# A second batch of attention in half heads, paired with the first

## The chip, the cores and the metric

The kernel runs on one core of a Trainium2 chip. The metric is device time in microseconds (us) of one execution. The engines are named as in the profile: PE (matrix multiply; PEld is its weight load), DVE (vector), ACT (scalar, activations), POOL (GpSimd) and SP (which issues DMAs). Each engine works through its own instructions in a fixed order and waits on semaphores for the others.

## The reference, cut to what matters

Eight batches of eight heads, 576 positions, head dimension 64. Attention with a decay, its output laid out as 4608 rows of 512, then two dense layers with a hard swish between:

```python
scores = scale * np.matmul(q, k.transpose(0, 1, 3, 2))
cum = np.cumsum(np.log(np.clip(f, 0.0001, 1.0)), axis=-1)
scores = np.where(causal, -1000000000.0, scores + cum[..., :, None] - cum[..., None, :])
attn = np.exp(scores - np.max(scores, axis=-1, keepdims=True))
attn = attn / (np.sum(attn, axis=-1, keepdims=True) + 1e-09)
x = np.matmul(attn, v).transpose(0, 2, 1, 3).reshape(B * S, H * D)
h = x @ w_in                                   # 512 -> 2048
g = h * np.clip(h + 3.0, 0.0, 6.0) / 6.0
return (g @ w_out).astype(np.float32)          # 2048 -> 512
```

The weights arrive in 64-bit floats and are decoded on the chip.

## The kernel before, in words

**Visits.** The program is one loop (L959) over a list of visits, `VH` (L96). A visit of kind "A" takes the first 256 query rows of two heads of batch 0 at once (4 visits). Kind "B" takes the other 320 query rows of one head of batch 0 (8 visits). Kind "F" takes a whole head; batches 1 to 7 go so (56 visits).

**Halves, A and B.** `natural` (L477) multiplies queries and keys once in float32 and takes each row's maximum on DVE (L493). `max_rows` turns the maxima into a row and sends it by DMA into the query tile. `scores` (L544) then computes the scores with keys on the partitions, in two matmuls (L551, L552) and a mask (L554), and ACT takes the exponential into a float32 tile. `av` (L682) multiplies this with V in float32 (L705). Each such matmul shows as two records. Its V is the unsplit one, and it reads a window of `NAV = 96` columns of it, which holds the head's 64 columns and its column of ones.

**Whole heads, F.** `rows` (L594) computes scores with queries on the partitions (L611, L614), takes the maximum on DVE while copying (L622), the exponential on ACT (L634), then splits the result into two float16 halves (L648, L651, L657, L662) and transposes it by DMA (L669). `av` multiplies it with a V that `v_split` has split into float16 halves (L694 to L699).

**The dense layers** come in units, a queue `units` that `done` (L936) fills when the eight heads (or the four pairs) of a batch are through and moved by `x_move` into a tile `xT` of 512 rows. `moe_in` computes h in 16 units (`h_unit`, L770: three float16 matmuls for each of four chunks, then L783, L786, L787, L788), `moe_out` the output in units of 128 rows (`out_unit`, L819: L824 to L826, accumulated over all 16 chunks). Batch 0 does this for its first 256 rows and then for the next 256; other batches for 512 rows at once. 64 rows of each batch are left, and two batches' rests go together (`rest_in`, `rest_out`). Two PSUM buffers (`ps_m`, L763) serve the h and output units, from batch 1 on also a third.

**Weights.** `w_in_work` and `w_out_work` are generators of about 85 steps: load, decode (L251 to L253), sum of squares, scale, split into float16 halves (L284, L287, L288, L295). Each visit takes `W_RATE` of them: 8 in A, 5 in B, 4 in F. The output units of batch 0 first run out what is left of them (L847).

**Order.** In each visit eight calls of `fill` (L925) put units in between the attention's instructions; a call earns `F_RATE` units (0.6 in B, 0.45 in batch 1, 1.06 later). Inputs are loaded three visits ahead, and copies to float32r tiles are made on POOL two ahead. The weighted sum of a visit is issued at the end of the next one, and `x_move` follows one visit later still. A scheduler with a model of the engines then fixes each engine's order.

Of the kernel before, what the change touches and what calls it, by code (L numbers as in the profile page):

```python
# [20 lines left out]
def kernel(  # L21
# [95 lines left out]
    def init_qk(i, eng):  # L117
# [5 lines left out]

    NAV = 96
    pav = ps_a.tile([P, NCH, NAV], F32, name="pav")

# [11 lines left out]

    v0 = [
        v16.bitcast(F32).rearrange("p n c j e -> p (n c j e)")[:, 0:3 * VR],  # L140
        xT[1].bitcast(F32).rearrange("p a c l t -> p (a c l t)")[:, 0:2 * VR],
    ]
    v0 = [t.rearrange("p (c e) -> p c e", e=VR) for t in v0]

    def v_parts(b):
        return v0 if b == 0 else [vst[:, 0:3], vst[:, 3:]]

    def v_chunk(b, c):
        return v_parts(b)[c // 3][:, c % 3]

# [199 lines left out]
    def load_v(b):  # L350
        src = vS[b]
        lo, hi = v_parts(b)
        with pinned() if PIN_V else nullcontext():
            if b == 0:
                nc.sync.dma_start(lo, src[0:3 * P].rearrange("(c p) e -> p c e", p=P))
                nc.sync.dma_start(hi[:, 0], src[3 * P:4 * P])
                nc.sync.dma_start(hi[:64, 1], src[4 * P:S])
            else:
                for p in (0, 64):
                    nc.sync.dma_start(vst[p:p + 64, 0], src[0:64])  # L360
                nc.sync.dma_start(vst[:, 1:], src[64:].rearrange("(c p) e -> p c e", p=P))

    def v_scale(b):
        pm = p2.tile([P, 2], F32, tag="pm", name=f"vm{b}")
# [8 lines left out]
        nc.vector.tensor_tensor(pm, pm, pm, op=ALU.mult)  # L373
        nc.vector.tensor_tensor(pm[:, 0:1], pm[:, 0:1], pm[:, 1:2], op=ALU.max)
        yield from pow2_scale(pm[:, 0:1], SV + b, IV + b, f"v{b}")
# [15 lines left out]
    def v_split(g):  # L391
        b, hp = divmod(g, NPAIR)
        t = v16[:, g % NV16]
        if g < NPAIR + NV16:
# [280 lines left out]

    def window(head):

        o = head % H * (D + 1)
        w0 = min(o, VR - NAV)
        return w0, o - w0  # L680

    def av(v, ph):  # L682
# [4 lines left out]
        if kind == "F":  # L687
            jh = n % 2
            blk = [(n, c, c) for c in range(NCH)]
            vh, vl = vt[:, :, jh, 0:D + 1], vt[:, :, jh, D + 1:VW]  # L690
            for c in range(NCH):
                pb = ph[:, HT[c]:HT[c] + (2 * c + 1) * P].rearrange("p (g t) -> p g t", t=P)
                o1, o0 = pav[:, c, 0:D + 1], pav[:, c, 0:D]
                nc.tensor.matmul(o1, pb[:, c], vh[:, 0], start=True, stop=False)  # L694
                nc.tensor.matmul(o0, pb[:, c], vl[:, 0], start=False, stop=(c == 0))
                for k in range(1, c + 1):
                    nc.tensor.matmul(o1, pb[:, c + k], vh[:, k], start=False, stop=False)
                    nc.tensor.matmul(o0, pb[:, c + k], vl[:, k], start=False, stop=False)  # L698
                    nc.tensor.matmul(o1, pb[:, k - 1], vh[:, k], start=False, stop=(k == c))  # L699
        else:  # L700
            blk = blocks(v)
            for head, c, pl, m, js in blk:
                w0, _ = window(head)
                for jc, o, kk in js:
                    nc.tensor.matmul(  # L705
                        pav[:m, pl, :], ph[:kk, o:o + m], v_chunk(b, jc)[:kk, w0:w0 + NAV],
                        start=(jc == 0), stop=(jc == c),
                    )
# [7 lines left out]
        for head in heads:  # L716
# [3 lines left out]
            c0, c1 = mine[0][1], mine[-1][1] + 1  # L720
            vo = window(head)[1] if b == 0 else 0
            rs = p2.tile([P, NCH, 1], F32, tag="rs", name=f"rs_{v}_{jh}")[:, p0:p1]
            total = pav[:, p0:p1, vo + D:vo + D + 1]
            if b == 0:

# [6 lines left out]
            nc.vector.tensor_tensor(  # L732
                xf[:, c0:c1, jh * D:(jh + 1) * D], pav[:, p0:p1, vo:vo + D],
                rs.to_broadcast([P, p1 - p0, D]), op=ALU.mult,
# [7 lines left out]
    def x_move(v):  # L742
# [12 lines left out]
        nc.sync.dma_start_transpose(  # L755
            xT[b % 2][:, cc, o:o + c1 - c0].rearrange("p c a t -> p (c a) t"),
            xhl[:, c0:c1].rearrange("p c a e -> p (c a e)"),
# [11 lines left out]

    def h_unit(x, fc, c0, c1, b, three, name):  # L770

# [3 lines left out]
        for cc in range(NCC):  # L775
# [6 lines left out]
        r = p2.tile([P, TT], F32, tag="rt", name=f"r_{name}_{fc}_{c0}", bufs=3)[:, :nw]  # L782
        nc.scalar.activation(  # L783
            r, ph, AF.Relu, bias=bias_r, scale=scol(A1 + NG * b + fc * NG // NFC)
        )
        nc.vector.scalar_tensor_tensor(r, r, 6.0 * CG, ph, op0=ALU.min, op1=ALU.mult)  # L786
# [49 lines left out]

    def moe_in(b, c0=0, c1=TT):

        for fc in range(NFC):
            j, new = divmod(fc, NFC // NG)  # L840
            if new == 0 and c0 == 0:
                while j not in w_in_done:
                    next(w_in_q, None)
                moe_scale_in(b, j)
            yield from h_unit(xT[b % 2], fc, c0, c1, b, b > 0 or c0 > 0, f"{b}")

    def moe_out(b, c0=0, c1=TT):  # L847

        if b == 0:
            for _ in wq:  # L850
                pass
        if c0 == 0:
            moe_scale_out(b)
        for s in range(c0 // P, c1 // P):
            r = S * b + (64 if b else 0) + s * P
            yield from out_unit(s, UO + b, [(r, r + P)], b > 0 or s * P >= QA, f"{b}")

# [8 lines left out]
    def rest_out(k, g):  # L866

        b = 2 * k
        r = S - 64 if b == 0 else S * b
        yield from out_unit(  # L870
            0, UX + b + 1, [(r, r + 64), (S * (b + 1), S * (b + 1) + 64)], True, f"r{k}", g
        )

# [62 lines left out]
    def done(v):  # L936
        kind, n = VH[v]
        if kind == "A":
            if n == NPAIR - 1:
                units.append(moe_in(0, 0, QA))  # L940
                units.append(moe_out(0, 0, QA))
            return
        b, h = divmod(n, H)
        if h == H - 1:
            cut = QA if b == 0 else 0
            units.append(moe_in(b, cut, TT))
            if b == B - 1:
# [11 lines left out]
    for i, (kind, n) in enumerate(VH):  # L959
        b, h = divmod(n, H)  # L960
        if kind == "A":
            b = h = 0
# [18 lines left out]
        fill(1)  # L981
        if b + 1 < B and h == 7:
            vq = v_scale(b + 1)
        next(vq, None)
        fill(1)
# [15 lines left out]
        fill(1)  # L1001
        if b + 1 < B and h == 7:
            for _ in vq:
                pass
            if b:
                v_split((n + 1) // 2)
# [7 lines left out]
        if prev is not None:  # L1014
            av(*prev)
            if VH[prev[0]][0] == "A" or VH[prev[0]][1] % 2 == 1:
                pend_x = prev[0]
        if n == H:
            v_split(n // 2)
# [45 lines left out]
```

## Time and profile before

| | |
|---|---|
| median of 3 runs | 1073.61 us (1069.77 to 1073.86) |
| the profiled execution, its own time | 1069.33 us |
| its span in the profile | 1067.5 us |
| busy in it: PE, DVE, ACT, POOL | 1006.3, 731.1, 587.3, 403.4 us |
| granted PE clock, mean | 0.988 |

The span runs from the first to the last instruction. "Busy" on PE counts modelled durations that reach into the next matmul; the distance between the starts of two matmuls is the better price where PE is full. A view by windows gives busy time in each stretch and, in brackets, the number of instructions; "PEclk" is the granted clock as a share of full speed.

### The profile page before, as it was taken

How to read it: one execution, taken by the hardware profiler on the slowest of the kernel's cores; microseconds unless marked ns; L12 is line 12 of the kernel's file. 1: busy time of each engine (PE TensorE's matmuls, PEld its weight loads, DVE VectorE, ACT ScalarE, POOL GpSimd, SP SyncE). 2: the span in 40 equal slices, each digit the busy share in tenths (PEclk: the TensorE clock that was granted, in tenths of full speed). 3: DMA queues.
4: the chain of work that ended last, by engine and by line, in shares of the span. 5: the costliest groups of instructions: out<-in, count | busy, mean ns of one | idle time of the engine just before them, and what ended most of it. 6: DMA issues, size and time to landing. Idle time of an engine off the chain costs nothing.

```text
span 1067.5 us, 21157 instructions
## 1 busy us (share of the span) xinstructions
PE 1006.3 (94%) x7650; PEld 598.0 (56%) x7650; DVE 731.1 (68%) x1887; ACT 587.3 (55%) x1189; POOL 403.4 (38%) x505
## 2 busy tenths in 40 slices
PE   2799977899999999999999999999999999999897
PEld 1577844665555755555555755555555755444543
DVE  6978899996876768866886668846895677105300
ACT  4778666764764557545654557635764566115301
POOL 8343466443443444344443444534443330000000
PEclk9989989999999999999999999999999999999999
DMA  8965647955856776667575766566557554010000
GB/s 240 308 187 194 151 109 145 220 114 118 169 116 134 139 153 124 113 148 165 118 134 118 158 140 119 118 136 167 119 112 145 103 100 74 12 40 1 1 20 30
DMA packets 259155, 133.78 MB, mean 125 GB/s; under 512 B 226948, under 2 KB 228540, under 8 KB 259052
## 3 DMA queue, kind: packets, MB, share of 16 engines
q1 hardware_dynamic: 259052, 132.44, 55.7%
q8 instruction: 60, 0.98, 0.4%
q14 instruction: 43, 0.35, 0.1%
HBM read 47.93 MB, written 9.73 MB: 54 GB/s over the span
## 4 chain that ended last, share of the span: by engine, by line
PE 76%; DVE 12%; ACT 5%; issue 4%; DMA 2%; POOL 1%; SPq 0%; DVEq 0%; ACTq 0%; POOLq 0%
PE po L824 9%; PE po L826 9%; PE po L825 9%; PE ph L777 9%; PE ph L778 9%; PE ph L779 9%; PE pn L611 3%; PE pn L614 3%; DVE pp L622 2%; DVE ring L651 2%; PE po_r L826 1%; PE pav L698 1%; ACT pp L634 1%; PE po_r L824 1%; PE po_r L825 1%
## 5 line engine op out<-in xcount | busy, mean ns | idle before, releaser
L634 ACT ACTIVATE pp<-pp,nb 128x192 f32<-128x192 f32 x280 | 138.6, 552 | 170.3 <-DVE nb L628 150.8
L777 PE MATMUL ph<-xT,w 128*128 128x512 f16 (+1 forms) x576 | 198.8, 357 | 2.5 <-DVE r L786 2.4
L825 PE MATMUL po<-w,gT 128*128 128x512 f16 x512 | 192.6, 382 | 8.0 <-DVE w L295 8.0
L779 PE MATMUL ph<-xT,w 128*128 128x512 f16 (+1 forms) x576 | 198.0, 356 | 0.0
L778 PE MATMUL ph<-xT,w 128*128 128x512 f16 (+1 forms) x576 | 197.8, 356 | 0.0
L651 DVE TENSOR_TENSOR ring<-pp,ring 128x128 f16<-128x128 f32 (+2 forms) x216 | 138.0, 650 | 85.6 <-ACT ring L648 84.7
L824 PE MATMUL po<-w,gT 128*128 128x512 f16 x512 | 190.4, 383 | 5.8 <-DVE r_r L813 2.7
L826 PE MATMUL po<-w,gT 128*128 128x512 f16 x512 | 192.4, 383 | 0.0
L622 DVE CUSTOM_DVE_ANT_0 pp<-pn,W 128x192 f32<-128x192 f32 x280 | 123.3, 482 | 29.3 <-PE pn L614 28.0
L461 POOL TENSOR_TENSOR T<-ST,T 64x576 fp32r<-64x576 f32 (+1 forms) x68 | 100.9, 1483 | 107.2 <-DMA T<-TK 85.8
L786 DVE SCALAR_TENSOR_TENSOR r<-r,ph 128x512 f32<-128x512 f32 (+1 forms) x144 | 89.1, 620 | 61.4 <-ACT r L783 60.6
L611 PE MATMUL pn<-TK,TQ 68*128 68x192 f32 x336 | 124.8, 385 | 3.8 <-issue 2.2
L788 DVE TENSOR_TENSOR gT<-r,gT 128x512 f16<-128x512 f32 (+1 forms) x144 | 111.6, 781 | 22.0 <-ACT gT L787 20.6
L614 PE MATMUL pn<-T,T 128*128 128x192 f32 x336 | 115.2, 368 | 0.2 <-POOL T L461 0.2
L783 ACT ACTIVATE r<-ph,bias_r,SC 128x512 f32<-128x512 f32 (+1 forms) x144 | 103.9, 725 | 19.2 <-PE ph L779 17.1
L648 ACT CAST ring<-pp 128x192 f16<-128x192 f32 x280 | 114.2, 449 | 0.0
L787 ACT CAST gT<-r 128x512 f16<-128x512 f32 (+1 forms) x144 | 81.4, 567 | 59.6 <-DVE r L786 59.3
L449 POOL TENSOR_SCALAR TK<-ST 64x576 fp32r<-64x576 f32 (+1 forms) x68 | 49.2, 724 | 167.8 <-PE pn L611 142.9
L657 POOL TENSOR_TENSOR ring<-pp,ring 128x128 f16<-128x128 f32 x96 | 61.0, 636 | 116.1 <-ACT ring L648 75.2
L458 POOL TENSOR_TENSOR T<-ST,TQ 64x576 fp32r<-64x576 f32 (+2 forms) x68 | 95.2, 1400 | 17.7 <-PE pn L614 11.1
L826 PEld LDWEIGHTS <-gT 128*128 128x128 f16 x560 | 54.8, 98 | 74.5 <-issue 15.1
L825 PEld LDWEIGHTS <-gT 128*128 128x128 f16 x560 | 54.9, 98 | 66.5 <-issue 11.9
(158 smaller groups left out, 2010.2 us busy)
## 6 DMA issues: line engine op xcount, KB each, us to landing
ST<-in_qk_dram SPq DMA_DIRECT2D x64, 288.0 KB
T<-TK SPq DMA_DIRECT2D x64, 144.0 KB
ring<-in_w_out_dram SPq DMA_DIRECT2D x16, 512.0 KB
out_dram<-o SPq DMA_DIRECT2D x32, 256.0 KB
T<-TQ SPq DMA_DIRECT2D x56, 144.0 KB
vst<-in_vS_dram SPq DMA_DIRECT2D x7, 1040.0 KB
ring<-in_w_in_dram SPq DMA_DIRECT2D x9, 512.0 KB
w<-in_w_in_dram SPq DMA_DIRECT2D x7, 512.0 KB
```

Of the source, the lines that this page charges most:

```text
L611: nc.tensor.matmul(dst, TQ[i][0:D + 4, qs], TK[i][0:D + 4, a:e], start=True, stop=False)
L614: nc.tensor.matmul(dst, T7[j][:, qs], T1[j][:, a:e], start=False, stop=True)
L622: nc.vector.tensor_tensor_reduce(pp[:r, w:w + kw], pn[:r, o:o + kw], W[:r, 4 * P + r - kw:4 * P + r], 1.0, -3.0e38, ALU.add, ALU.max, accu ...
L634: nc.scalar.activation(x_, x_, AF.Exp, bias=nb[:r, e0 + x:e0 + x + 1], scale=0.125)
L648: nc.scalar.copy(hl[:r, h0[c]:h0[c] + kw], pp[:r, at[c]:at[c] + kw])
L651: eng.tensor_tensor(hl[:r, a:a + c * P], pp[:r, at[c] + 64:at[c] + kw], hl[:r, h0[c] + 64:h0[c] + kw], op=ALU.subtract,)
L777: nc.tensor.matmul(ph, w1[0][:, cc, fs_], xh, start=(cc == 0), stop=False)
L778: nc.tensor.matmul(ph, w1[0][:, cc, fs_], xl, start=False, stop=False)
L779: nc.tensor.matmul(ph, w1[1][:, cc, fs_], xh, start=False, stop=(cc == NCC - 1))
L824: nc.tensor.matmul(po, g[:, 0, fc, ts_], w2[:, fc, 0, :], start=(fc == 0), stop=False)
L825: nc.tensor.matmul(po, g[:, 0, fc, ts_], w2[:, fc, 1, :], start=False, stop=False)
L826: nc.tensor.matmul(po, g[:, 1, fc, ts_], w2[:, fc, 0, :], start=False, stop=(fc == NFC - 1))
```

## The change

Batch 1 is taken like batch 0. `VH` becomes 8 A visits (pairs of batches 0 and 1), 16 B visits and 48 F visits. The first halves of both batches share the tile `xT[0]` and 512 rows of `gT`, the second halves share `xT[1]`. The first halves' h units are still made per batch, 256 rows each; the second halves' are made for both at once, with one activation for each batch's 256 columns. V of batch 0 now lies in `vst`; V of batch 1 lies in `v16` and, chunks 3 and 4, in two tiles of the tag "Pp", which the F visits' L622 writes later. `NAV` becomes 65. The weighted sum of the last B visit is issued at the beginning of the first F visit instead of its end. V of batch 1 is loaded in the second A visit, V of batch 2 in the second B visit of batch 1. A unit earns 0.45 in A, 0.36 in B and 1.06 in F; weight steps are 8, 5 and 5 a visit.

```diff
-    VH = [("A", g) for g in range(NPAIR)] + [("B", n) for n in range(H)]
-    VH += [("F", n) for n in range(H, NHEAD)]
+    NB2 = 2
+    VH = [("A", g) for g in range(NB2 * NPAIR)] + [("B", n) for n in range(NB2 * H)]
+    VH += [("F", n) for n in range(NB2 * H, NHEAD)]
...
-    NAV = 96
+    NAV = D + 1
...
+    v1 = v16.bitcast(F32).rearrange("p n c j e -> p (n c j e)")[:, 0:3 * VR]
+    v1 = [v1.rearrange("p (c e) -> p c e", e=VR)]
     def v_parts(b):
-        return v0 if b == 0 else [vst[:, 0:3], vst[:, 3:]]
+        return v1 if b == 1 else [vst[:, 0:3], vst[:, 3:]]
...
+            if b < NB2:
+                for c, r in ((3, P), (4, 64)):
+                    if b:
+                        t = p2.tile([P, 832], F32, tag="Pp", name=f"v1_{c}")[:, 0:VR]
...
-            if b == 0:
+            if kind != "F":
                 nc.vector.tensor_scalar(
                     rs, total, PSC * 1e-9, scol(IV + b), op0=ALU.add, op1=ALU.mult
...
+        o = 0 if kind == "F" else CA * b
+        x = xT["AB".index(kind) if kind != "F" else b % 2]
...
+        hw = nw // len(bs)
+        for i, b in enumerate(bs):
+            o = slice(i * hw, (i + 1) * hw)
+            nc.scalar.activation(
+                r[:, o], ph[:, o], AF.Relu, bias=bias_r,
...
-            if n == NPAIR - 1:
-                units.append(moe_in(0, 0, QA))
-                units.append(moe_out(0, 0, QA))
+            b, h = divmod(n, NPAIR)
+            if h == NPAIR - 1:
+                units.append(moe_in(xT[0], [b], True, QA * b, QA * b + QA))
+                if b:
+                    units.append(moe_out(0, "A"))
+                    units.append(moe_out(1, "A"))
...
+            if b < NB2:
+                units.append(moe_in(xT[1], [0, 1], False))
+                units.append(moe_out(0, "B"))
+                units.append(moe_out(1, "B"))
...
-        wn = W_RATE["ABF".index(kind)]
-        rates[0] = F_RATE[0] if kind == "B" else F_RATE[min(b, 2)]
+        late = kind == "F"
+        wn = (8, 5, 5)["ABF".index(kind)]
+        rates[0] = F_RATE[2] if late else (0.36, 0.36)[b] if kind == "B" else 0.45
...
+        if kind == "A" and (b, h) == (0, 1):
+            load_v(1)
+        if kind == "B" and (b, h) == (1, 1):
+            load_v(2)
...
+        if late and not (b, h) > (NB2, 0):
+            av(*prev)
+            prev = None
```

More of the change, by code (lines that the diff above doesn't have):

```diff
@@ L363, in v_scale @@
     def v_scale(b):
-        pm = p2.tile([P, 2], F32, tag="pm", name=f"vm{b}")
+        pm = p2.tile([P, 3], F32, tag="pm", name=f"vm{b}")
+        n = len(v_parts(b))
         for i, t in enumerate(v_parts(b)):
@@ L372, in v_scale @@
             yield
[L373 to L374 removed]
+        nc.vector.tensor_tensor(pm[:, 0:n], pm[:, 0:n], pm[:, 0:n], op=ALU.mult)
+        for i in range(1, n):
+            nc.vector.tensor_tensor(pm[:, 0:1], pm[:, 0:1], pm[:, i:i + 1], op=ALU.max)
         yield from pow2_scale(pm[:, 0:1], SV + b, IV + b, f"v{b}")
@@ L674 @@
     xpair = {}
[L676 to L680, printed above, removed]
     def av(v, ph):
@@ L702, in av @@
             for head, c, pl, m, js in blk:
-                w0, _ = window(head)
+                w0 = head % H * NAV
                 for jc, o, kk in js:
@@ L720, in av @@
             c0, c1 = mine[0][1], mine[-1][1] + 1
-            vo = window(head)[1] if b == 0 else 0
             rs = p2.tile([P, NCH, 1], F32, tag="rs", name=f"rs_{v}_{jh}")[:, p0:p1]
-            total = pav[:, p0:p1, vo + D:vo + D + 1]
-            if b == 0:
+            total = pav[:, p0:p1, D:D + 1]
+            if kind != "F":
                 nc.vector.tensor_scalar(
@@ L732, in av @@
             nc.vector.tensor_tensor(
-                xf[:, c0:c1, jh * D:(jh + 1) * D], pav[:, p0:p1, vo:vo + D],
+                xf[:, c0:c1, jh * D:(jh + 1) * D], pav[:, p0:p1, 0:D],
                 rs.to_broadcast([P, p1 - p0, D]), op=ALU.mult,
@@ L768, in mm_tile, with h_unit @@
         return ps_m.tile([P, TT], F32, tag="mm", name=name)
-    def h_unit(x, fc, c0, c1, b, three, name):
+    def h_unit(x, fc, c0, c1, bs, three, name):
         nw = c1 - c0
@@ L835, in out_unit, with moe_in, moe_out @@
         yield 2.0 - H_COST
-    def moe_in(b, c0=0, c1=TT):
+    def moe_in(x, bs, first, c0=0, c1=TT):
         for fc in range(NFC):
             j, new = divmod(fc, NFC // NG)
-            if new == 0 and c0 == 0:
+            if new == 0 and first:
                 while j not in w_in_done:
                     next(w_in_q, None)
[L844 to L849, printed above, removed]
+                moe_scale_in(bs[0], j)
+            yield from h_unit(x, fc, c0, c1, bs, c1 - c0 == TT, f"{bs[-1]}_{c1 - c0}")
+    def moe_out(b, kind):
+        if b == 0 and kind == "A":
             for _ in wq:
                 pass
-        if c0 == 0:
+        if kind != "B":
             moe_scale_out(b)
-        for s in range(c0 // P, c1 // P):
-            r = S * b + (64 if b else 0) + s * P
-            yield from out_unit(s, UO + b, [(r, r + P)], b > 0 or s * P >= QA, f"{b}")
+        for s in range(TT // P if kind == "F" else CA):
+            r = S * b + {"A": 0, "B": QA, "F": 64}[kind] + s * P
+            yield from out_unit(
+                s + (CA * b if kind != "F" else 0), UO + b, [(r, r + P)], kind != "A",
+                f"{kind}{b}",
+            )
     g_end = vst.bitcast(F16).rearrange("p c e -> p (c e)")[:, 0:2 * NFC * P]
@@ L868, in rest_out @@
         b = 2 * k
[L869 to L872, printed above, removed]
+        rows = [S * i + (S - 64 if i < NB2 else 0) for i in (b, b + 1)]
+        yield from out_unit(0, UX + b + 1, [(r, r + 64) for r in rows], True, f"r{k}", g)
     dec = decay()
@@ L981 @@
         fill(1)
-        if b + 1 < B and h == 7:
+        if kind != "A" and b and b + 1 < B and h == 7:
             vq = v_scale(b + 1)
+        if kind == "A" and (b, h) == (0, 3):
+            for _ in vq:
+                pass
+            vq = v_scale(1)
         next(vq, None)
@@ L1001 @@
         fill(1)
-        if b + 1 < B and h == 7:
+        if kind == "A" and (b, h) == (1, 0) or kind != "A" and b and b + 1 < B and h == 7:
             for _ in vq:
                 pass
-            if b:
+            if late:
                 v_split((n + 1) // 2)
@@ L1015 @@
             av(*prev)
-            if VH[prev[0]][0] == "A" or VH[prev[0]][1] % 2 == 1:
-                pend_x = prev[0]
-        if n == H:
+        if i and (VH[i - 1][0] == "A" or VH[i - 1][1] % 2 == 1):
+            pend_x = i - 1
+        if late and n == NB2 * H:
             v_split(n // 2)
```

43 lines of the change are left out of this document (21 added, 22 removed).

## The prediction

> **What bounds the kernel now.** I read the page's first line, then busy time by stage, then the order of time on PE, then DVE's groups.
>
> ```profile
> span 1067.5 us, 21157 instructions
> ```
>
> Which engine lacks work, and where? The stages: first halves of batch 0 (20 to 64 us), its second halves (64 to 141), batch 1 in full heads (141 to 249), the 48 later heads (249 to 907).
>
> ```profile
> core 0: us, PE busy (x) PEld busy (x) DVE busy (x) ACT busy (x) POOL busy (x), PEclk, DMA share, GB/s
> 20.00:64.00 44.00, 33.92 (x147) 25.21 (x147) 36.40 (x111) 31.24 (x66) 17.66 (x18) 0.88 0.85 266
> 64.00:141.00 77.00, 74.33 (x574) 61.99 (x573) 66.13 (x190) 54.15 (x113) 35.33 (x38) 1.00 0.63 175
> 141.00:200.00 59.00, 43.43 (x372) 25.58 (x371) 57.48 (x147) 38.74 (x83) 37.60 (x34) 0.88 0.70 149
> 200.00:249.00 49.00, 46.22 (x407) 32.19 (x405) 38.20 (x107) 29.31 (x69) 15.87 (x19) 1.00 0.69 142
> 249.00:907.00 658.00, 656.24 (x5319) 377.98 (x5316) 487.89 (x1250) 387.34 (x785) 278.93 (x363) 1.00 0.63 130
> ```
>
> From 249 to 907 us PE stands still for 658.0 - 656.2 = 1.8 us. So any PE work put into this kernel comes back as time, and only an early PE gap can be won. After 64 us the gaps are 2.7 + 15.6 + 2.8 = 21.1 us, and the granted clock of 0.88 from 141 to 200 us costs another 0.12 x 59 = 7.1: **28.2 us are all that can be won.** The 15.6 has a cause:
>
> ```profile
> 145.20 0.58 PE L825 MATMUL po<-w,gT 128*128 128x512 f16 x1 [3.80 <-DVE w L295]
> ```
>
> The output units of batch 0's first half wait for w_out to be split on DVE (L295), holding both L763 buffers, while DVE (57.5 of 59 us) also has the full heads of batch 1.
>
> **The change, part by part.**
>
> *Step 1, PE work.* Eight full heads ("F") become four pairs of first halves ("A") and eight second halves ("B"). A matmul's duration here is modelled and has a tail that overlaps the next one, so I price by the distance between starts.
>
> ```profile
> 109.15 0.42 PE L551 MATMUL ps<-TQ,TK 97*128 97x320 f32 x1
> 109.40 0.31 PE L552 MATMUL ps<-T,T 128*128 128x320 f32 x1
> 109.55 0.31 PE L551 MATMUL ps<-TQ,TK 97*128 97x320 f32 x1
> ...
> 109.94 0.38 PE L705 MATMUL pav<-xT,pf 64*64 64x96 f32 x2
> ...
> 112.88 0.40 PE L551 MATMUL ps<-TQ,TK 97*128 97x320 f32 x1
> ...
> 113.63 0.28 PE L551 MATMUL ps<-TQ,TK 97*128 97x64 f32 x1
> 113.74 0.28 PE L552 MATMUL ps<-T,T 128*128 128x64 f32 x1
> ...
> 114.08 0.68 PE L487 MATMUL pn<-TK,TQ 66*128 66x512 f32 x2
> 114.60 0.58 PE L705 MATMUL pav<-v,pf 128*128 128x96 f32 x4
> ...
> 117.56 0.51 PE L487 MATMUL pn<-TK,TQ 66*64 66x128 f32 x2
> 117.90 0.58 PE L705 MATMUL pav<-v,pf 128*128 128x96 f32 x4
> ...
> 135.47 1.47 PE L705 MATMUL pav<-v,pf 128*128 128x96 f32 x12
> 136.78 0.39 PE L705 MATMUL pav<-xT,pf 128*128 128x96 f32 x2
> 137.09 0.71 PE L705 MATMUL pav<-v,pf 128*64 128x96 f32 x6
> 137.64 0.63 PE L705 MATMUL pav<-xT,pf 128*64 128x96 f32 x4
> 138.21 0.28 PE L777 MATMUL ph<-xT,w 128*128 128x256 f16 x1
> 138.33 0.27 PE L778 MATMUL ph<-xT,w 128*128 128x256 f16 x1
> ```
>
> A B head: maximum pass L487 0.52 + 0.34 = 0.86; scores 0.79 (109.15 to 109.94) + 1.20 (112.88 to 114.08) = 1.99; weighted sum L705 138.21 - 135.47 = 2.74: 5.6 us. The first matmul of a group stands 0.25 from the next, the others 0.15; without eight such starts it is 4.8. I take 5.2. An A pair has 12 records of L705 (136.78 - 135.47 = 1.31), 768 columns of L487 and 1536 of scores against a B head's 1472 and 2432: 1.31 + 0.86 x 768/1472 + 1.99 x 1536/2432 = 3.0, and with masks and starts up to 3.6; I take 3.3. Batch 1 costs 8 x 5.2 + 4 x 3.3 = 54.8 us instead of:
>
> ```profile
> 153.68 0.34 PE L611 MATMUL pn<-TK,TQ 68*128 68x192 f32 x1
> ...
> 154.56 0.22 PE L614 MATMUL pn<-T,T 128*64 128x64 f32 x1
> 154.62 0.39 PE L825 MATMUL po<-w,gT 128*128 128x512 f16 x1
> ...
> 155.93 0.19 PE L694 MATMUL pav<-v,pT 128*128 128x65 f16 x1
> ...
> 156.15 0.39 PE L611 MATMUL pn<-TK,TQ 68*128 68x320 f32 x1
> ...
> 156.94 0.39 PE L825 MATMUL po<-w,gT 128*128 128x512 f16 x1
> ```
>
> An F head: 0.94 + 0.79 for the scores, and 40 f16 matmuls (L694 to L699) at (156.15 - 155.93) / 7 = 0.031: 1.25. Together 3.0, times 8 = 24. So +30.8.
>
> The window of 65 instead of 96 columns takes some back, in both batches. A 64-column matmul on 128 float32 weight columns stands 0.11 from the next (113.63 to 113.74), as does a 96-column one (1.31/12): there 65 columns win nothing. With 64 weight columns the distance is 0.55/6 = 0.09 now and 0.06 for L614's 64 columns (154.56 to 154.62): ten such records in a second half (6 + 4 above), 80 a batch, 160 x 0.03 = 4.8 us. Bounds: nothing, and 480 records x 0.11 x 31/96 = 17 if all scaled. I take 4.8, since the 113.63 row is the same form. **Step 1: +26 us, from +10 to +35.** (The Trainium skill, "TensorE: Matmul & The Clock Gate", section LDWEIGHTS, has a load cost its columns divided by 1.2 GHz whatever the matmul streams, 107 ns for 128; the 0.11 agrees, and by it the narrow window is worth the same 4.8 and not 17.)
>
> The shared tiles win no PE time: first halves still run 256 columns at a time (two calls), second halves 512, as batch 1 did; weights are fetched as often. The L783 activations split for two batches, 16 more on ACT, which is at 38.7 of 59 us even in the crowded stage: nothing.
>
> *Step 2, what becomes free.* Output units of the first half now come after 33.6 units of h work instead of 16.8, when the splits are over: the L295 wait and its stage go, -28.2 at most (gaps and low clock of 64 to 249 us). On DVE:
>
> ```profile
> L493 DVE CUSTOM_DVE_ANT_0 junk<-pn,W 128x512 bf16<-128x512 f32 (+2 forms) x18 | 11.9, 661 | 3.0 <-PE pn L487 2.8
> ...
> L788 DVE TENSOR_TENSOR gT<-r,gT 128x256 f16<-128x256 f32 x16 | 10.3, 653 | 1.2 <-ACT gT L787 1.2
> ...
> L786 DVE SCALAR_TENSOR_TENSOR r<-r,ph 128x256 f32<-128x256 f32 x16 | 6.5, 408 | 0.3 <-ACT r L783 0.3
> ```
>
> Above are groups of 64 to 141 us (second halves), below of 141 to 249 (full heads of batch 1):
>
> ```profile
> L651 DVE TENSOR_TENSOR ring<-pp,ring 128x128 f16<-128x128 f32 (+3 forms) x28 | 18.2, 662 | 1.7 <-ACT ring L648 1.5
> L622 DVE CUSTOM_DVE_ANT_0 pp<-pn,W 128x192 f32<-128x192 f32 (+4 forms) x40 | 17.5, 477 | 0.2
> ```
>
> So 18.2 + 17.5 = 36 us of DVE leave with the full heads, and the second halves bring 11.9 of L493.
>
> *Step 3, four more A visits.* They keep 8 weight steps each, so steps 33 to 64 (the rest of w_in, all decoding of w_out) leave the PE-heavy B visits, where 74.3 of 77 us were covered, for A visits that have 3.3 us of PE work. The first four show the pace:
>
> ```profile
> 35.62 0.22 DVE L726 TENSOR_SCALAR rs<-pav,SC 128x2 f32<-128x2 f32 x1
> ...
> 64.01 0.20 DVE L726 TENSOR_SCALAR rs<-pav,SC 128x2 f32<-128x2 f32 x1
> ```
>
> Three visits in 28.4 us, 9.5 each, DVE at 36.4 of 44. The new four carry about 9 h units besides (fills of 0.45, units from the sixth visit on), each 0.653 + 0.408 = 1.06 us of DVE: 4 x 9.5 + 9.5 = 47.5 us. PE has 4 x 3.3 for the halves and 9 units of 12 matmuls 0.12 apart (138.21 to 138.33), 1.4 each: 26. **Gap 20, from 6 (weights slip back under B) to 30** (what is left of w_in's products on PE covers some of the difference of 21.5); a clock of 0.88 as in 20 to 64 us takes 3 more.
>
> *Step 4, the rest.* The next four B visits hold the splits: 4 us. Twelve B visits of some 9 us at the 2.7/77 gap of today's: 4. The first F visit: batch 1's V chunks 3 and 4 sit in the two "Pp" buffers, so its L622 waits for the last B's L705, which is moved ahead of it; behind L622 on DVE stand the L786 of h units, whose L763 buffers PE then lacks. Units queued from the halves cover most of it: 2, from 0 to 5. Batch 1's V moves to the second A visit:
>
> ```profile
> vst<-in_vS_dram SPq DMA_DIRECT2D x7, 1040.0 KB
> ```
>
> At 266 GB/s that is 4 us where the DMA share is 0.85: 1, from 0 to 4. Its scale (the L366 reductions) moves with it, the same instructions. On SP's queue an F head puts about 8 transfers, two of them P transposes (16 in the batch, gone), an A pair or a B head 6: 64 become 72, and SP has no part in any gap above.
>
> *Rates.* Before, about 31 units run in B and 29 in batch 1; now 9 in A and 46 in B. The 5 fewer run later on a full PE, inside the total: nothing.
>
> **Sum** against the profiled execution (1069.33 us, span 1067.5 plus 1.8): +26 - 28 + 20 + 3 + 4 + 4 + 2 + 1 = +32: **1101 us**. The median of the runs lies 4 us above that execution; I leave the sum where it is, since one run in three matched it.
>
> **Rivals.**
> *Gaps close.* The full heads' DVE load goes, the weight steps slip under the B visits, and PE stands still 6 us at most from 64 us on: with step 1 at +16, 16 - 28 + 6 = -6: **1063**. For it: the 36 us of DVE that leave. Against: the decoding sits in visits that have little PE work by their make. It turns the sign only where step 1 plus all new gaps stay under 28. (The Trainium skill, "Perfetto Trace Analysis", section Optimization Strategy, says that interleaving regimes with different contended engines may help. That is this rival; the 64 to 141 us row shows such an interleaving already there.) Chance 0.12.
> *A wash:* step 1 at +16, gaps of 7 in the A visits, 3 for their clock, 4 after: 16 - 28 + 7 + 3 + 4 = +2: **1071**. 0.08.
> *Worse:* the A visits wait for DVE throughout, with gaps of 30, and step 1 at +35, the first F visit at 5, V's load at 4: 35 - 28 + 30 + 3 + 8 + 5 + 4 = +57 at the extreme; half way from the forecast, +45: **1114**. 0.18.
> *It doesn't do what it says:* a shared tile could double the columns per weight load; the two calls of 256 rule that out for first halves, and second halves only keep 512. No separate time.
>
> **The numbers.** Forecast 0.62, worse 0.18, wash 0.08, gaps close 0.12. Range 1072 to 1118: it leaves out most of the gaps-close case and the extreme of the worse one. A measurement here tells 0.5% (5 us) from no change: faster 0.12, same 0.08, slower 0.80.
>
> **What would show it.** Step 1: L705 480 records, L611 288; L705's 128-weight records still 0.11 apart. Step 2: no L825 wait on L295 of microseconds. Step 3: PE at 50 to 65% in the four visits after 64 us, DVE near 90%. Step 4: first full head near 270 us, then PE full to the end. I am wrong if PE is covered in the second four A visits, or L705 gets a third cheaper.

## The result and the profile after

| | before | after |
|---|---|---|
| median of the runs | 1073.3 us (1069.77 to 1073.86) | 1096.74 us (1091.91 to 1100.62) |
| the profiled execution | 1069.33 us | 1098.46 us |
| its span, its mean granted clock | 1067.5 us, 0.988 | 1096.7 us, 0.982 |

The changed kernel is slower: the ratio is 1.0228, with a 95% interval of 1.0202 to 1.0253. That is 23 us by the medians and 29 by the two profiled executions. The forecast was 1101 us, slower with a chance of 0.80.

The first rows of the page of the changed kernel show PE still filling 95% of the span, DVE with less to do than before, and, of the 336 L611 records, 288 left (now line 617):

```profile
span 1096.7 us, 21170 instructions
...
PE 1041.8 (95%) x7686; PEld 626.9 (57%) x7686; DVE 705.5 (64%) x1858; ACT 570.3 (52%) x1141; POOL 406.5 (37%) x505
...
L617 PE MATMUL pn<-TK,TQ 68*128 68x320 f32 (+4 forms) x288 | 109.9, 394 | 0.0
```

The stages of the changed kernel, in the same view by windows as in the prediction: first A visits to 64 us, a handover to 73, the second four A visits (73 to 123), 16 B visits (123 to 268), and the 48 full heads (268 to 932):

```profile
core 0: us, PE busy (x) PEld busy (x) DVE busy (x) ACT busy (x) POOL busy (x), PEclk, DMA share, GB/s
20.00:64.00 44.00, 33.45 (x146) 23.66 (x146) 33.95 (x109) 30.59 (x63) 19.71 (x19) 0.96 1.01 278
64.00:73.00 9.00, 6.06 (x30) 5.62 (x30) 9.00 (x38) 5.22 (x13) 4.08 (x5) 0.55 0.90 265
73.00:123.00 50.00, 41.41 (x267) 31.88 (x267) 37.66 (x120) 33.71 (x74) 20.45 (x19) 0.84 0.54 158
123.00:195.00 72.00, 71.27 (x594) 59.44 (x593) 59.83 (x156) 42.40 (x82) 31.79 (x33) 1.00 0.29 69
195.00:268.00 73.00, 73.00 (x481) 50.27 (x481) 29.43 (x98) 17.47 (x27) 28.79 (x32) 1.00 0.38 100
268.00:932.00 664.00, 660.34 (x5297) 379.21 (x5295) 490.26 (x1255) 393.74 (x809) 283.61 (x368) 1.00 0.63 130
```

The stage of 141 to 200 us, in which PE stood for 15.6 of 59 us, has no counterpart: from 123 us on PE is covered. In its place stand the second four A visits, with PE idle for 8.6 us at a clock of 0.84, and the handover ahead of them at 0.55.

PE's busy time can't be compared directly, since durations at half clock count double. So I price every matmul at the usual distance to the next start where PE is full (0.216 us for 512 float16 columns, 0.112 and 0.059 for a record of L705 on 128 and on 64 weight columns, and so on). The sum is PE's work; what is left of a stage is lost time: idle, slow clock, and the small delays at the first matmul of a group, which no window shows as a gap:

| | before | after |
|---|---|---|
| PE work in all | 972.3 us | 994.4 us |
| lost, 0 to 64 us | 42.5 | 42.0 |
| lost, 64 us to the end of the half heads' and first full heads' stages | 9.6 + 22.5 + 4.0 = 36.1 (to 249) | 5.8 + 17.7 + 7.7 + 5.9 + 4.6 = 41.7 (to 300) |
| lost after that | 17.1 | 18.9 |

So 22 of the 29 us are more work on PE and 7 are more lost time. The totals hang on which distance is called usual; with the median, the lower quartile or a mean without the long ones instead, the added work comes to 24, 24.5 or 21 us. What was lost with batch 1's full heads was won, and somewhat more was lost anew.

The 7 us are not more standing: span less busy time of PE is 1067.5 - 1006.3 = 61.2 us before and 1096.7 - 1041.8 = 54.9 after. What grew is the slow clock, by the mean granted clocks at most 0.012 x 1067.5 = 12.8 us before and 0.018 x 1096.7 = 19.7 after, and the small delays.

### The profile page after: what moved, and what is told of

Read it like the earlier page. It is cut to its first block, busy times and chain, and to the rows that moved or that the text cites. A ratio compares the mean times of both kernels' runs of the same rounds, so it can differ in the third digit from the quotient of the medians.

```text
span 1096.7 us, 21170 instructions
## 1 busy us (share of the span) xinstructions
PE 1041.8 (95%) x7686; PEld 626.9 (57%) x7686; DVE 705.5 (64%) x1858; ACT 570.3 (52%) x1141; POOL 406.5 (37%) x505
## 3 DMA queue, kind: packets, MB, share of 16 engines
q1 hardware_dynamic: 234804, 127.33, 51.3%
## 4 chain that ended last, share of the span: by engine, by line
PE 83%; DVE 7%; ACT 3%; DMA 3%; issue 2%; POOL 1%; SPq 0%; ACTq 0%; POOLq 0%; DVEq 0%
PE ph L777 9%; PE ph L779 9%; PE ph L778 9%; PE po_F L828 7%; PE po_F L830 7%; PE po_F L829 7%; PE pav L705 4%; PE pn L620 3%; PE pn L617 3%; DMA ring<-in_w_out_dram 2%; PE po_r L830 1%; PE po_r L828 1%; PE pav L698 1%; PE po_r L829 1%; PE po_B L828 1%
## 5 line engine op out<-in xcount | busy, mean ns | idle before, releaser
L640 ACT ACTIVATE pp<-pp,nb 128x192 f32<-128x192 f32 (+4 forms) x240 | 118.8, 552 | 165.0 <-DVE nb L634 145.0
L777 PE MATMUL ph<-xT,w 128*128 128x512 f16 (+1 forms) x576 | 201.4, 361 | 3.1 <-DMA xT<-xhl 2.7
L779 PE MATMUL ph<-xT,w 128*128 128x512 f16 (+1 forms) x576 | 200.5, 360 | 0.0
L778 PE MATMUL ph<-xT,w 128*128 128x512 f16 (+1 forms) x576 | 200.4, 360 | 0.0
L657 DVE TENSOR_TENSOR ring<-pp,ring 128x128 f16<-128x128 f32 x192 | 123.5, 655 | 84.1 <-ACT ring L654 83.4
L828 PE MATMUL po_F<-w,gT 128*128 128x512 f16 x384 | 143.9, 382 | 4.4 <-DVE r_r L817 2.7
L467 POOL TENSOR_TENSOR T<-ST,T 64x576 fp32r<-64x576 f32 (+1 forms) x72 | 105.5, 1467 | 108.9 <-DMA T<-TK 106.1
L829 PE MATMUL po_F<-w,gT 128*128 128x512 f16 x384 | 143.6, 381 | 0.0
L830 PE MATMUL po_F<-w,gT 128*128 128x512 f16 x384 | 143.2, 381 | 0.0
L628 DVE CUSTOM_DVE_ANT_0 pp<-pn,W 128x192 f32<-128x192 f32 (+4 forms) x240 | 105.7, 483 | 29.0 <-PE pn L620 26.4
L792 DVE TENSOR_TENSOR gT<-r,gT 128x512 f16<-128x512 f32 (+1 forms) x144 | 106.2, 743 | 21.2 <-ACT gT L791 19.6
L617 PE MATMUL pn<-TK,TQ 68*128 68x320 f32 (+4 forms) x288 | 109.9, 394 | 0.0
L620 PE MATMUL pn<-T,T 128*128 128x320 f32 (+4 forms) x288 | 101.4, 377 | 0.0
L654 ACT CAST ring<-pp 128x192 f16<-128x192 f32 (+4 forms) x240 | 98.1, 449 | 0.0
L829 PEld LDWEIGHTS <-gT 128*128 128x128 f16 x560 | 55.0, 98 | 64.9 <-issue 9.6
```

Source lines behind the costliest of these rows:

```text
L617: nc.tensor.matmul(dst, TQ[i][0:D + 4, qs], TK[i][0:D + 4, a:e], start=True, stop=False)
L620: nc.tensor.matmul(dst, T7[j][:, qs], T1[j][:, a:e], start=False, stop=True)
L640: nc.scalar.activation(x_, x_, AF.Exp, bias=nb[:r, e0 + x:e0 + x + 1], scale=0.125)
L657: eng.tensor_tensor(hl[:r, a:a + c * P], pp[:r, at[c] + 64:at[c] + kw], hl[:r, h0[c] + 64:h0[c] + kw], op=ALU.subtract,)
L777: nc.tensor.matmul(ph, w1[0][:, cc, fs_], xh, start=(cc == 0), stop=False)
L778: nc.tensor.matmul(ph, w1[0][:, cc, fs_], xl, start=False, stop=False)
```

## The experiments

All times are set beside runs of the kernel before on the same chip (medians 1071.18, 1071.22 and 1070.49 us in the three groups). A difference from the changed kernel is taken from the medians (its own is 1096.74). By its ratio of 1.0228 it would stand at 1095.6, 1095.6 and 1094.9 us beside the three groups, so such a difference is uncertain by 1 to 2 us.

### Is the added PE work the cost, one for one?

Three runs put work in or take it out. The first takes work out of the changed kernel: for batch 1's halves it multiplies only the first chunk of keys with V, so 160 of the 480 records of L705 are left out and that part of the output isn't computed.

```diff
+                if b == 1:
+                    js = js[:1]
                 for jc, o, kk in js:
```

> The changed kernel, leaving out part of batch 1's weighted sums: each block of its half heads sums over its first chunk of keys only (160 of 240 L705 records less, 96 at 0.11 and 64 at 0.06 us, 14.4 us of PE work, nearly all in the B visits of 195 to 268 us, where PE shows no gap). Theory (the loss is PE work, which is time one for one): faster than the changed kernel by 12 to 17 us, 1080 to 1085. Rival (the B visits keep their 9 us by another bound, and PE only looks busy): faster by 0 to 5 us.

It took 1083.9 us (ratio 1.0117, 1.0098 to 1.0136), 12.8 less than the change, for 14.3 us less PE work by starts; lost time, priced as above, stayed at 101.9 us against 102.6. Work in the half heads came back nearly one for one.

The second puts work into the kernel before, where PE is full: 800 more float16 matmuls of 65 columns among the weighted sums of batches 3 and 4.

```diff
+                if g // NPAIR in (3, 4):
+                    for _ in range(10):
+                        nc.tensor.matmul(o1, pb[:, c], vh[:, 0], start=True, stop=True)
```

> The kernel before with 800 more float16 matmuls of 65 columns in the weighted sums of batches 3 and 4 (each block's first one is made eleven times over, the result is the same): 25 us of PE work at 0.031 each, in the stretch of about 390 to 610 us where PE is full. Theory (PE work there is time one for one): slower by 20 to 30 us, 1091 to 1101. Rival (the units of the dense layers only wait less at later boundaries): slower by under 10 us.

It took 1094.44 us (ratio 1.0231, 1.02 to 1.0261): +24.0 for 800 x 0.031 = 24.8 us. In the full stage work is time.

The third doubles batch 0's float32 weighted sums in the kernel before.

```diff
-                for jc, o, kk in js:
+                for jc, o, kk in js + js:
```

> The kernel before, with each weighted sum of batch 0's half heads (L705) computed twice over the same place: 240 more records, 160 at 0.11 and 80 at 0.09 us, 25 us of PE work in the stages of 20 to 141 us. Theory (PE is full from 64 us on, so that its work there is time one for one; only the A visits' share of 5 us can hide): slower by 18 to 26 us, 1091 to 1100. Rival (the half heads have slack on PE, and the change's loss is its A visits alone): slower by 0 to 8 us.

It took 1109.34 us (ratio 1.0339, 1.0298 to 1.0381): +38 for 24.4 us of work, and here one for one failed. The windows of this run, for the other 14:

```profile
70.00:160.00 90.00, 88.65 (x673) 71.05 (x672) 60.94 (x160) 52.38 (x107) 27.59 (x31) 1.00 0.42 123
160.00:225.00 65.00, 57.33 (x473) 43.91 (x473) 49.88 (x140) 36.48 (x79) 27.87 (x28) 0.87 0.49 103
225.00:326.00 101.00, 88.03 (x709) 54.35 (x708) 82.55 (x230) 61.66 (x134) 48.69 (x59) 0.90 0.78 165
```

The B visits are covered (1.35 us of gaps), and behind them PE stands for 7.7 and 13.0 us. These 22.0 us are hardly more than the 21.1 of the kernel before from 64 to 249 us. What is new is the clock of 0.87 and 0.90: it takes at most 0.13 x 65 + 0.10 x 101 = 18.6 us, where the same estimate for before gave 7.1. So most of the 14 goes with the slow clock. Why gaps of the same sum drew more of it stays open; that the added work kept units back, which batch 1's full heads then met in another order, is argued and not shown. The largest wait there is this one, for a transposed x:

```profile
PE ph L777 <- DMA xT<-xhl: 7.7, 3, 3.0
```

So work put into a full stage can cost more than itself, when the stages behind it then run at a slower clock.

### Is the narrow window worth 4.8 us, or 17?

The changed kernel with 96 columns again for each head, the window placed so that it ends within the tile.

```diff
-    NAV = D + 1
+    NAV = 96
...
-                w0 = head % H * NAV
+                w0 = min(head % H * (D + 1), VR - NAV)
...
-            total = pav[:, p0:p1, D:D + 1]
+            total = pav[:, p0:p1, vo + D:vo + D + 1]
```

> The changed kernel with the 96-column window of before in the weighted sums, in both batches. Theory (128 float32 weight columns set 0.11 us whatever is streamed; only the 64-column records pay, 0.03 each, 160 of them): slower by 2 to 6 us, 1098 to 1103, and the 128-weight records stand 0.11 apart in both. Rival (the records scale with their columns): slower by 12 to 17 us, 1109 to 1114.

It took 1095.53 us (1093.46 to 1099.3, ratio 1.0224, 1.0185 to 1.0264), against 1.0228 with the narrow window. A saving of 17 is ruled out; 4.8 isn't seen either, though an interval of 0.4% to each side doesn't rule out a few us. The trace itself gives the sizes. In the changed kernel's order of time on PE, 12 records of 65 columns stand between these starts:

```profile
45.74 1.45 PE L705 MATMUL pav<-vst,pf 128*128 128x65 f32 x12
47.00 0.36 PE L558 MATMUL ps<-T,T 128*128 128x256 f32 x1
```

1.26 / 12 = 0.105 us each, against 1.31 / 12 = 0.109 with 96 columns before. With 64 weight columns the median distance fell from 0.083 to 0.059: 160 such records make 3.8 us. In the run with 96 columns it is 0.082 again.

### Is it the weights' decoding that opens the second A visits?

The first try took fewer weight steps in these visits.

```diff
-        wn = (8, 5, 5)["ABF".index(kind)]
+        wn = 4 if kind == "A" and b else (8, 5, 5)["ABF".index(kind)]
```

> The changed kernel, with 4 instead of 8 weight steps in each of batch 1's four A visits; nothing else. Theory (those visits wait for DVE because the decoding is packed into them, and PE's gaps and its half clock follow from that): the stretch of the second four A visits, 73 to 123 us with 8.6 us of PE gaps and a granted clock of 0.84, shortens by 8 to 16 us, the decoding goes on in B visits, and the whole comes to 1080 to 1090 us. Rival (an A visit is slow by its own chain of copies, maxima and loads, with or without weights): the stretch keeps its 12.5 us a visit and the time stays within 1093 to 1100 us. Third: in the B visits, where PE is full, the weights' DVE work delays the half heads, and the time rises.

It took 1097.23 us (ratio 1.0235, 1.02 to 1.0271): no change against the changed kernel, and it tells nothing about the weights, because they did not move. The groups on DVE from 73 to 123 us, first of the changed kernel:

```profile
L251 DVE SCALAR_TENSOR_TENSOR w<-ring,w 128x512 int32<-128x512 int32 x12 | 9.6, 798 | 0.1
...
L250 DVE TENSOR_SCALAR w<-w 128x512 int32<-128x512 int32 x11 | 6.8, 624 | 6.3 <-ACT w L249 6.1
```

then of this experiment:

```profile
L251 DVE SCALAR_TENSOR_TENSOR w<-ring,w 128x512 int32<-128x512 int32 x13 | 9.1, 698 | 0.0
...
L250 DVE TENSOR_SCALAR w<-w 128x512 int32<-128x512 int32 x12 | 7.1, 593 | 5.1 <-ACT w L249 5.1
```

13 decodings instead of 12 stand in the same stretch. The scheduler fixes each engine's order, so presumably it put them back where it had found room before.

The second leaves work out: the two DVE instructions that complete the decoding of w_out (22 us in all), so w_out stays partly undecoded in it.

```diff
-            nc.vector.tensor_scalar(i32, i32, 3, None, op0=ALU.logical_shift_left)
-            nc.vector.scalar_tensor_tensor(
-                i32, lo, 29, i32, op0=ALU.logical_shift_right, op1=ALU.bitwise_or
-            )
+            if i == 0:
+                nc.vector.tensor_scalar(i32, i32, 3, None, op0=ALU.logical_shift_left)
+                nc.vector.scalar_tensor_tensor(
+                    i32, lo, 29, i32, op0=ALU.logical_shift_right, op1=ALU.bitwise_or
+                )
```

> The changed kernel, leaving out the two DVE operations that decode w_out (16 x 1.4 = 22 us of DVE in the stretch of 64 to 123 us; the output is wrong by it). The run with fewer weight steps in these visits did not move the decoding (12 and 13 of L251 in 73 to 123 us), so it could not tell this. Theory (the second four A visits wait for DVE): they take 9 to 10 us each instead of 12.5, PE's gap falls from 8.6 to under 4 us, and the whole gets faster by 8 to 15 us, to 1082 to 1089. Rival (they wait for their own chain of maxima, copies and exponentials): 11.5 to 12.5 us a visit, faster by 0 to 4 us.

It took 1079.01 us (ratio 1.0071, 1.0054 to 1.0089), 17.7 less than the change. The second four A visits lie from 70.0 to 97.8 us now, 6.9 us each instead of 12.5; the 4 x 5.6 us are as much as the 22 us of DVE that were left out. The windows of this run:

```profile
64.00:73.00 9.00, 9.00 (x34) 6.75 (x35) 4.51 (x26) 4.80 (x9) 2.83 (x4) 0.52 0.96 272
73.00:110.00 37.00, 35.52 (x292) 30.55 (x291) 27.08 (x101) 30.20 (x68) 17.29 (x21) 1.00 0.84 222
110.00:183.00 73.00, 72.60 (x598) 60.33 (x597) 56.48 (x154) 44.82 (x87) 27.07 (x31) 1.00 0.33 85
```

PE's gap from 73 to 110 us is 1.5 us and the clock stays at 1.00. The second A visits were held by the decoding on DVE, as step 3 said, and by more than the run was expected to show.

The third keeps the decoding and moves it under the B visits: it is held behind the maxima of half heads, and only two steps are taken in a second A visit.

```diff
+            with tc.issue_after(last_max[-1]):
+                w_decode(1, k, slots_out)
...
+            last_max[:] = [d.ins]
...
-        wn = (8, 5, 5)["ABF".index(kind)]
+        wn = 2 if kind == "A" and b else (8, 6, 5)["ABF".index(kind)]
```

> The changed kernel with the decoding of w_out held behind the maxima of its visit in DVE's order, 2 weight steps in batch 1's A visits and 6 in B: all of w_out's decoding now stands behind the 40th of 80 maxima (the A visits have 32), where before 15 of 16 stood ahead of it. Nothing is left out. Theory (the second four A visits last as long as DVE has decoding to do, and the B visits, DVE 60 of 72 us and then 29 of 73, have room): A visits take 7 to 9 us each, the B visits up to 1 us more, and the time falls by 8 to 15 us, to 1082 to 1089. Rival (the decoding costs its 22 us wherever it stands, since PE has to wait for w_out or the half heads for DVE): 1093 to 1100.

It took 1092.65 us (ratio 1.0209, 1.0183 to 1.0236), 4 us less than the change by the medians and 2 by the ratios, whose intervals overlap, and not the 18 of the run before it. The windows of this run, over the second A's with the first B's, and over the next ones:

```profile
73.00:123.00 50.00, 46.30 (x390) 40.08 (x389) 45.90 (x136) 30.75 (x66) 20.78 (x21) 1.00 0.46 122
123.00:195.00 72.00, 68.40 (x480) 55.91 (x479) 59.11 (x149) 48.28 (x97) 26.23 (x29) 0.86 0.49 136
```

The second A visits took 6.5 us each (the fourth pair's last sum is done at 95.7 us instead of 122.8), but the next eight B visits took 11.9 instead of 9.0, and the loss from 123 to 195 us rose from 7.7 to 18.6 us. Of these, 3.6 are standing and at most 0.14 x 72 = 10.1 slow clock. The loss moved with the decoding. (The Trainium skill, "Perfetto Trace Analysis", section Optimization Strategy, says that interleaving regimes with different contended engines may help. Here it gave back 4 us of 18 at most.)

### Was the wait for w_out's split the cause of the old gap?

Step 2 named L825's wait for L295 as the cause of the 15.6 us before. Three runs of the kernel before try it without the second batch's change. The first queues the output units of the first half behind the h units of the second, so that w_out is ready for them.

```diff
                 units.append(moe_in(0, 0, QA))
-                units.append(moe_out(0, 0, QA))
...
+            if b == 0:
+                units.append(moe_out(0, 0, QA))
             units.append(moe_out(b, cut, TT))
```

> The kernel before, with batch 0's first-half output units queued after its second-half h units instead of ahead of them. It tests by itself what the change was credited with in step 2: outputs no longer hold both L763 buffers while w_out is being split. Theory (the 15.6 us gap of 141 to 200 us is that wait): no L825 wait on L295 of microseconds is left, the gap falls to 5 us or less, and the time falls by 5 to 15 us, to 1058 to 1068. Rival (the gap is DVE's, 57.5 of 59 us busy with the full heads of batch 1 and the splits, and PE would find nothing else to do): the wait goes, but the gap stays as other short waits on DVE, and the time stays within 1068 to 1076.

It took 1099.8 us (ratio 1.0265, 1.023 to 1.0299), slower by 28.6. The wait for L295 is gone, but not the gap. The windows of this run, and PE's longest waits from 146 to 245 us (line waited for: us in all, times, longest):

```profile
146.00:203.00 57.00, 38.88 (x384) 31.91 (x383) 53.80 (x152) 41.98 (x93) 33.57 (x29) 0.82 0.72 139
...
640.00:720.00 80.00, 69.25 (x504) 38.03 (x502) 67.81 (x165) 50.46 (x102) 38.21 (x48) 0.94 0.58 122
```

```profile
PE pn L611 <- DVE MF L622: 5.8, 2, 5.3
PE pn L611 <- issue: 5.7, 1, 5.7
PE pav L694 <- DMA pT<-ring: 4.7, 3, 2.4
PE pav L694 <- DVE xf L732: 2.6, 1, 2.6
```

PE stands for 18.1 us in the stage where DVE is busy 53.8 of 57: with batch 1's full heads there, another wait comes in the place of the one removed. And a new gap of 10.8 us stands at 640 to 720, hundreds of us behind the edit; that the units kept back make it is argued, not shown.

The second gives every other split of w_out's rest to POOL.

```diff
-    POOL_REST = ((0, 0, 0, 0), (0, 0, 0, 0))
+    POOL_REST = ((0, 0, 0, 0), (1, 0, 1, 0))
```

> The kernel before, with every second w_out chunk's lower half computed on ACT and POOL instead of DVE (8 of 16 L295 at 0.82 us go, 6.6 us of DVE; ACT gets 8 copies of 0.7). It tests what the 15.6 us of PE gap from 141 to 200 us wait for, since with the outputs queued later the L295 wait was gone and 18 us of gap stayed. Theory (DVE, 57.5 of 59 us busy, is the bound of that stage): the gap falls by 4 to 8 us, the time by 3 to 8, to 1063 to 1069. Rival (ACT and POOL are as tied into the chain of a full head, or POOL holds up DVE): no change within 3 us, or slower.

It took 1091.03 us (ratio 1.0182, 1.0158 to 1.0207), slower by 20. The same unit waits, now for the other engine (before: L825 on L295, 8.0 us in four times), and the gap of 141 to 200 us is 19.7 us at a clock of 0.83, though DVE has 50.3 us of work there instead of 57.5:

```profile
PE po L825 <- POOL w L293: 12.6, 4, 9.8
```

```profile
141.00:200.00 59.00, 39.26 (x336) 24.94 (x335) 50.31 (x133) 39.64 (x83) 42.74 (x41) 0.83 0.67 139
```

The third takes the weight steps earlier, 7 instead of 5 in a B visit and with a smaller distance.

```diff
-    W_RATE = (8, 5, 4)
+    W_RATE = (8, 7, 4)
...
-    W_GAP = 5
+    W_GAP = 1
```

> The kernel before with 7 instead of 5 weight steps in a B visit and 1 instead of 5 empty steps ahead of w_out's scale: the 16 splits (L295) start some two full heads earlier in DVE's order, the first before any full head. Theory (the gap of 141 to 200 us is the splits falling among the full heads, and they would be covered under B visits): the gap falls from 15.6 to 5 to 10 us, the time by 4 to 10, to 1061 to 1067. Rival (DVE has no room under the B visits either, 66 of 77 us): the B visits grow by what the gap loses, no change within 4 us.

Ten runs have a median of 1066.77 us (1064.94 to 1076.12) beside 1070.49 of thirteen runs of before: ratio 0.9984, 0.9958 to 1.0009, not told from no change. The profile was taken in the quickest of the ten runs. In it, the wait for L295, and the stages of 64 to 249 us:

```profile
PE po L825 <- DVE w L295: 4.3, 4, 2.1
```

```profile
64.00:141.00 77.00, 72.90 (x545) 59.04 (x545) 63.98 (x175) 52.67 (x111) 36.42 (x39) 1.00 0.62 171
141.00:200.00 59.00, 49.19 (x459) 33.39 (x458) 57.17 (x165) 43.82 (x97) 37.21 (x34) 1.00 0.75 152
200.00:249.00 49.00, 46.17 (x388) 30.25 (x386) 39.16 (x117) 27.17 (x62) 19.20 (x23) 1.00 0.69 156
```

The wait halves, from 8.0 us, and the gap of 141 to 200 us goes from 15.6 to 9.8, with 4.1 instead of 2.7 us ahead of it; the clock there is 1.00 instead of 0.88. So the wait had a part in the gap. That the rest is DVE's load, still 57 of 59 us, is argued and not shown: in the run with POOL the gap grew with less load on DVE, as the wait for the split grew too.

### Does the load of batch 1's V cost the first A visits?

In the changed kernel the last sum of batch 0's A visits is done at 72.7 us instead of 65.0. This run loads V of batch 1 two visits later, and takes its scale one visit later.

```diff
-        if kind == "A" and (b, h) == (0, 1):
+        if kind == "A" and (b, h) == (0, 3):
             load_v(1)
...
-        if kind == "A" and (b, h) == (0, 3):
+        if kind == "A" and (b, h) == (1, 0):
```

> The changed kernel with batch 1's V loaded two A visits later, and its scale one later. Theory (the 1040 KB among the weights at a DMA share of 1.0 delay the first A visits: last weighted sum of batch 0's at 72.7 us instead of 65): that sum comes at 66 to 70 us and the time falls by 2 to 6 us. Rival (the first visits are late for another reason, or the 7 us are made up by then): no change beyond 2 us.

It took 1095.55 us (ratio 1.0221, 1.0205 to 1.0236), 1.2 less than the change, and the same sum is done at 73.6 us. The load isn't what makes it late. In the run without w_out's decoding the same sum is done at 70.0 us and in the one with the decoding held back at 69.5, so some 3 of the 7.7 us go with that decoding; what makes the rest stays open.

## Why the prediction was right

Against the kernel's own profiled execution the sum said +32 us and +29.1 came. By the medians it was +23, so the forecast lies 4 above the median. By its terms, with the priced work and lost time of both traces:

| term | predicted | measured |
|---|---|---|
| step 1, PE work | +26 | 994.4 - 972.3 = +22.1 |
| step 2, lost time that goes (64 to 249 us) | -28 | -36.1 |
| step 3, second A visits (64 to 123 us) | +20 + 3 | 5.8 + 17.7 = +23.5 |
| step 4, the rest (123 to 300 us) | +4 + 4 + 2 + 1 | 7.7 + 5.9 + 4.6 = +18.2 |
| outside these | 0 | 18.9 - 17.1 - 0.5 = +1.3 |
| sum | +32 | +29.0 |

The second and the fourth row are each off by 7 to 8 us, in opposite ways. The prediction counted gaps and clock of the windows, and the prices find the small delays at the starts of groups besides, in the old stages as in the new. By the prediction's own measure step 4 would have come to about 5 us instead of 11: 0.7 us of gaps from 123 to 268 us, 2.8 from 268 to 300, and at most 0.05 x 32 = 1.6 of slow clock there. So the sum is close in part by luck: gaps that didn't come stood in for small delays that had no term of their own.

**Step 1, PE work: right in kind, 4 too high.** L705 has 480 records and L617 288, as listed. The 240 more records of L705 cost 44.8 - 24.4 = 20.4 us, close to 240 times their predicted distances. Most of the 4 lie in the choice of 5.2 us for a B head between 4.8 without the slow group starts and 5.6 with them: priced without them, the step gives 8 x 0.4 = 3 less, and they stand in the fourth row instead. That this work is time was shown by taking 14.3 us of it away (-12.8) and by adding 24.8 elsewhere (+24.0); 24.4 added ahead of the full heads of batch 1 cost more, 38. The narrow window didn't change the 128-weight records (0.105 against 0.109) and made the 64-weight ones shorter by 0.024 instead of 0.03, as a sum 3.8 instead of 4.8; its effect on the time wasn't measurable.

**Step 2, what becomes free: right in size, its cause named too narrowly.** The gap and the slow clock of the old stages did go: from 123 us on no L829 waits for a split, and PE's longest waits from 64 to 268 us in the changed kernel are single ones for other things:

```profile
PE ps L557 <- DVE gT L792: 3.9, 1, 3.9
PE pn L493 <- ACT pf L576: 3.5, 1, 3.5
PE ps L557 <- DMA TQ<-mr: 2.0, 1, 2.0
```

But "the 15.6 has a cause", the output units that wait for L295, did not stand alone. Without that wait the gap was 18.1 us, with the split on POOL 19.7 (59.00 - 39.26 busy in the same stage), with earlier splits 9.8. The change took both away, the early output units and the full heads' 36 us of DVE, and no run takes away the full heads alone. That their leaving did most of it is argued from these three runs, not shown. "All that can be won" was too strong: the prices put 36.1 us into those stages, most of the difference in small delays that no window shows. The 7.1 us of slow clock in the 28.2, on the other hand, is an upper value, since it counts standing too; on the 43.4 busy us it is 0.12 x 43.4 = 5.2.

**Step 3, four more A visits: right, and shown.** The visits were put at 47.5 us. The last sums of the fourth and the eighth A visit in the changed kernel stand at:

```profile
72.65 0.15 DVE L730 RECIPROCAL rs<-rs 128x2 f32<-128x2 f32 x1
...
122.80 0.15 DVE L730 RECIPROCAL rs<-rs 128x2 f32<-128x2 f32 x1
```

So 50.2 us, 12.5 each. The loss was put at 20 + 3; from 64 to 123 us it is 5.8 + 17.7 = 23.5. By starts PE works 32.3 of the 50 us, 65%, the top of the 50 to 65 listed. Its division was off: PE's idle time by the windows is 8.6 + 2.9 = 11.5 us, where 20 had been put, and the half clock takes most of the rest, at most 0.16 x 50 + 0.45 x 9 = 12, where 3 had been put. That these two misses cancel is luck. DVE was to be near 90%: it is busy 37.7 of 50 us (75%) and stands 6.1 more in the decoding itself, which waits in a row for ACT and for the load of the weights. DVE's and ACT's waits from 73 to 123 us:

```profile
DVE w L250 <- ACT w L249: 6.1, 5, 2.0
```

```profile
ACT w L249 <- DMA ring<-in_w_out_dram: 7.2, 5, 2.0
```

With these 6.1 it is 88%. Each engine works in its own order, so the weighted sums' and the maxima's instructions behind such a wait wait too. The bound of 6, "weights slip back under B", was tried: they can be put there, and the loss goes with them.

**Step 4, the rest: B's gaps put too high, the first F visit's wait another one.** The B visits had been given 4 + 4 us of gaps; by the windows PE stands for 0.73 us from 123 to 268 us, at full clock, so that no gap of the predicted kind is there. By the prices 13.6 us of these 145 are lost, a smaller share than the 9.6 of 77 in the B visits before: small delays, which step 1's 5.2 us had in part. The handover to the full heads was put at 2, for a wait of L622's; it cost 4.6 through another one, for the transposed x of an h unit, with a slow clock behind it:

```profile
283.91 0.58 PE L777 MATMUL ph<-xT,w 128*128 128x512 f16 x1 [2.69 <-DMA xT<-xhl]
```

```profile
268.00:300.00 32.00, 29.23 (x207) 16.01 (x204) 22.64 (x53) 20.11 (x46) 16.24 (x19) 0.95 0.57 112
```

The sum of the first full head comes 19.3 us after the last B's (287.82 against 268.50); before it was 22.7 (164.01 against 141.33). V's load gives nothing back when it is later. As the loss of 0 to 64 us is unchanged (42.5 and 42.0), the later end of the first A visits shows only in the 64 to 73 us row.

**The rivals.** "Gaps close" wanted PE covered in the second four A visits: it was not. The trial of it, with the decoding under B, was still slower than before by 2.1%. "A wash" took 14 us of new losses on work of +16; the two rows of the table are 41.7 on +22. "Worse" took B at its upper bound and visits that wait throughout: neither came.

## What to carry to other kernels

Price a matmul by the distance between starts where the engine is full, and sum: it gave +22 where the busy times of the two pages say 1041.8 - 1006.3 = +35.5. Where an engine is full for most of the span, added work on it is time, and only early gaps can pay for it; a change that moves the load of a second engine (here DVE, by full heads out and decoding in) moves the loss with it. Count the slow clock beside the gaps: here it was as large. A wait that ends last in a crowded stage is not yet the stage's cause: take that one wait away by itself before counting the whole gap on it.

## What the runs showed of the hardware

A record of a float32 matmul on 128 weight columns takes 0.105 to 0.112 us from start to start with 65 or 96 columns alike, and on 64 weight columns 0.059 with 65 and 0.083 with 96: the first does not follow the streamed columns, the second does.

The slow clock took about as much as the idle time that it goes with. From 64 to 73 us the granted clock was 0.55 and from 73 to 123 0.84, while PE stood for 2.9 and 8.6 us; that makes at most 12 us of clock (standing in the slow stretches is counted in it too) for 11.5 of gaps. Without the decoding the clock was 1.00 from 73 to 183 us. The standing ahead of a slow stretch can be short: in the changed kernel the clock was at half from 51.3 us, and PE had been busy for 1.93 of the 3.4 us ahead of that:

```profile
47.90:51.30 3.40, 1.93 (x18) 1.76 (x17) 3.40 (x15) 2.80 (x6) 2.62 (x2) 0.99 1.45 378
51.30:54.70 3.40, 3.40 (x11) 2.37 (x11) 2.73 (x11) 3.40 (x7) 0.00 (x0) 0.50 1.11 68
```

(The Trainium skill, "TensorE: Matmul & The Clock Gate", section What's actually happening, has the clock at half rate after an idle window of about 3.4 us and back after a busy one. The lengths of the half-rate stretches of the changed kernel, 3.4 to 13.7 us, fit such windows; that PE must stand for a whole one does not, by the rows above.)

A small move shows up far from its place: output units queued later in the kernel before, at some 150 us, went with a new gap of 10.8 us at 640 to 720. Why the first A visits end 7.7 us later was found only in part: some 3 of them go with w_out's decoding.
